# Another order of work for the second layer of an attention and two-layer network kernel on one Trainium2 core

## The chip, the core and the metric

The kernel runs on one core of a Trainium2 chip. The metric is the device time of one execution in microseconds (us), as the median of several runs.

## The reference

The program computes local attention with block summaries, a gated first layer, and a normalized second layer with a residual. Only the second layer (`_moe2_ref`) is touched by the change, and the tail of the first layer where the second one begins:

```python
def _moe2_ref(x, g_ln, w_ch1, w_ch2):        # x: (2, 768, 512), w_ch1: (512, 2048), w_ch2: (2048, 512)
    mu = np.mean(x, axis=-1, keepdims=True)
    var = np.mean((x - mu) ** 2, axis=-1, keepdims=True)
    xn = (x - mu) / np.sqrt(var + 1e-06) * g_ln
    ch = np.maximum(xn @ w_ch1, 0.0) @ w_ch2
    return (x + ch).astype(np.float32)
```

## The kernel before

All work is cut into 1932 operations (`Plan.op`). A table at the head of the file, `ORDER`, gives them in one list: a number names the operation, the letter behind it its engine (P TensorE, V VectorE, A ScalarE, G GpSimd, S the queue that issues DMAs). `Plan.trace` (L128) writes the instructions out in that order, so each engine runs its operations strictly as they follow in the list, and waits where an input or a buffer is not ready. Nothing else sets the order. Numbers in fp32 are split into a high and a low part, and each product of two matrices is made from three matmuls (high by high, low by high, high by low).

The second layer goes in 16 steps: step n takes one of the two batches and one of eight slices of 256 hidden columns (`steps`, L1055). A step has two halves.

- **First products** (`step`, L1251; `product`, L1257; matmuls at L1264). The 512x256 slice of the first weight is multiplied with the normalized input by a scheme of seven half-size products in place of eight, numbered 0 to 6. Each is six matmuls of 384 columns into one PSUM bank named `ch`. There are two such banks. Each product is taken out of its bank by VectorE (`plus`, L1273, instructions at L1275, sums into the tiles `p` and `u`). Product 0 is only copied out (L1297, by VectorE at L243 or by ScalarE at L241, as the list says), and product 4 is read twice. A bank is free for the next product when its readers are done.
- The sums go through a relu (`block`, L1280): ScalarE writes the high part of `cb` (L1284), VectorE the low part (L1287).
- **Second products** (`accum`, L1308; matmuls at L1342). `cb` is multiplied with 256 rows of the second weight: six tiles of 128 tokens, six matmuls of 512 columns each, summed over the steps of a batch in six PSUM banks `acc`. At the end of a stretch of steps VectorE adds them to the residual (L1351); the very last tile is done in two pieces (L1326, L1333).

Beside these run the weights: each slice is loaded in raw form (`raw`, two buffers, L1067), made fp32 by VectorE (L619, L628) and ScalarE (L623), scaled (L1094, L1096), summed (L1108), and split into high (ScalarE, L1120 to L1142) and low (`low`, L1073, L1075, GpSimd or VectorE). At the start of the layer the last tiles of the first layer come out of PSUM with their row sums (ScalarE, L803), the negated means are made (L245 or L241), ScalarE squares the rows (L810), and `ln_stats` (L1040) makes the scale: VectorE L1044, GpSimd L1047, VectorE L1049. Then the rows are normalized (`xn`, L1167 on ScalarE, L1170 on VectorE) and transposed by TensorE (L1205) for the second batch. A "row" below is a run of products of one kind that follow each other on TensorE.

Of the kernel before, what the change touches and what calls it, by code (L numbers as in the profile page):

```python
# [41 lines left out]
1236V 1246P 1199A 1198V 1237A 1072V 1200V 1250P 1140A 1247V 1201A 1141V 1238V 1143P 1211A 1203V 1142P 1204A 1215V 1248A 1254P 1205V 1155A 1249V 1144A 1206V
1277P 1156A 1145V 1207V 1255A 1146V 1149A 1279P 1209V 1208V 1213A 1210G 1251V 1219S 1212A 1148V 1217G 1158P 1150V 1252A 1157P 1151A 1147V 1278P 1253V 1153A
1152V 1170A 1216V 1256P 1214A 1154V 1225S 1159A 1258P 1218G 1171A 1257V 1160V 1244A 1172P 1161V 1164A 1173P 1163G 1259V 1262P 1162V 1166A 1245V 1264P 1168A
1263V 1167G 1165V 1221A 1269P 1266V 1260A 1169G 1265V 1179A 1281P 1174A 1270V 1227A 1180V 1267A 1220V 1273P 1175V 1176V 1178G 1283P 1274V 1177V 1226V 1287P
1183A 1261V 1222V 1280P 1228V 1223A 1184V 1229A 1282P 1284A 1224V 1271A 1230V 1275A 1352S 1285P 1181A 1272V 1347S 1268V 1310P 1276V 1286V 1182V 1306P 1288V
1353V 1289A 1311V 1354A 1291P 1316P 1292V 1349A 1290V 1348V 1293P 1350V 1355V 1298P 1351G 1295V 1356A 1294V 1314P 1299V 1300A 1302P 1301V 1307V 1318P 1361A
1365V 1357V 1312P 1319A 1303V 1359G 1358V 1304A 1360G 1362A 1320P 1315V 1296A 1366V 1326P 1305V 1398S 1297V 1403S 1342P 1321V 1313V 1327V 1328P 1308P 1329V
1400A 1330V 1364A 1399V 1322P 1317V 1368G 1337P 1323V 1324A 1344P 1338V 1331A 1401V 1363A 1339A 1404V 1346P 1367G 1325V 1402A 1405A 1333P 1406V 1343P 1309V
# [20 lines left out]
1912P 1879V 1892P 1913P 1893V 1884P 1898P 1885V 1894A 1903P 1900V 1901A 1916P 1904V 1895V 1905A 1899V 1914P 1906V 1907P 1922P 1908V 1909A 1915P 1910V 1902V  # L70
1911P 1920P 1924P 1921V 1918P 1925V 1926P 1919V 1917V 1930P 1923V 1928P 1927V 1931V 1929V
"""


# [1363 lines left out]
```

## Time and profile before

| what | value |
|---|---|
| median of 3 runs | 471.58 us (471.5 to 471.64) |
| the profiled execution, its own time | 471.01 us |
| its span from the first to the last instruction | 469.3 us |
| TensorE, matmuls | 460.1 us busy, 98% |
| VectorE | 352.4 us, 75% |
| ScalarE | 253.8 us, 54% |
| GpSimd | 140.6 us, 30% |

In the profile, PE is TensorE's matmuls and PEld its weight loads, DVE is VectorE, ACT is ScalarE, POOL is GpSimd. A matmul's time there is from its start to a modelled end; matmuls overlap, so what one costs is the distance from its start to the next one's start. A timeline row gives its start, its length, and in brackets the idle time ahead of it with what ended that.

### The profile page before, as it was taken

To read this page: it belongs to the slowest core of one execution; us is meant where nothing else is said; L and a number is where in the kernel's file an instruction comes from. 1 tells how busy PE (TensorE), PEld (TensorE's weight loads), DVE (VectorE), ACT (ScalarE), POOL (GpSimd) and SP (SyncE) were. 2 spreads that over 40 slices of the span, in tenths; PEclk is the share of its full clock that TensorE was granted. 3 is DMA by queue.
4 is the path that set the end of the run, shared out by engine and by line. 5 is a ranking of instruction groups with operands and counts; after the bars stand their busy time and mean duration, and the time that the engine had idled before them with its cause. 6 is when DMAs were issued, how large, how long until landed. Compare 5 with 4: busy or idle time off the path is not lost.

```text
span 469.3 us, 8641 instructions
## 1 busy us (share of the span) xinstructions
PE 460.1 (98%) x3212; PEld 405.9 (86%) x3212; DVE 352.4 (75%) x700; ACT 253.8 (54%) x665; POOL 140.6 (30%) x179
## 2 busy tenths in 40 slices
PE   8989999999999999999999999999999999999996
PEld 5548999888899989988889899999898998998985
DVE  3998998998767857998999874677655677654643
ACT  2898998957766666968953432232343234322010
POOL 5354245562425244231513321131131332102000
PEclk9999999999999999999999999999999999999999
DMA  8999976433002202002221041202222022110203
GB/s 231 315 243 260 237 186 159 98 70 81 10 18 47 92 1 89 2 0 91 91 91 54 36 135 53 83 14 77 89 91 88 3 89 90 45 46 0 104 32 134
DMA packets 56062, 43.16 MB, mean 92 GB/s; under 512 B 34393, under 2 KB 46965, under 8 KB 56021
## 3 DMA queue, kind: packets, MB, share of 16 engines
q1 hardware_dynamic: 55876, 42.55, 32.3%
q8 instruction: 25, 0.41, 0.4%
q14 instruction: 17, 0.13, 0.1%
q10 hardware_dynamic: 144, 0.07, 0.1%
HBM read 39.22 MB, written 3.15 MB: 90 GB/s over the span
## 4 chain that ended last, share of the span: by engine, by line
PE 88%; DMA 4%; DVE 2%; SPq 2%; ACT 1%; POOL 1%; issue 1%; POOLq 0%; ACTq 0%
PE acc L1342 27%; PE ch L1264 23%; PE x L794 12%; PE h L717 6%; PE tr L717 5%; PE ch L717 4%; PE tr L479 3%; PE h L794 2%; DMA wst<-in_moe_w_in_dram 2%; PE tr L562 2%; PE tr L463 2%; PE tr L343 1%; SPq L323 1%; POOL wi L640 1%; PE tr L455 1%
## 5 line engine op out<-in xcount | busy, mean ns | idle before, releaser
L1342 PE MATMUL acc<-w,cb 128*128 128x512 f32 x570 | 138.1, 390 | 0.0
L1342 PEld LDWEIGHTS acc<-w,cb 128*128 128x128 f32 x570 | 106.4, 188 | 18.5
L1264 PE MATMUL ch<-xb,w 128*128 128x384 f32 x384 | 75.2, 337 | 0.0
L1264 PEld LDWEIGHTS ch<-xb,w 128*128 128x128 f32 x384 | 67.9, 188 | 2.3
L1275 DVE TENSOR_TENSOR u<-ch,u 128x384 f32<-128x384 f32 x64 | 34.9, 552 | 30.5 <-PE ch L1264 29.8
L1264 PE MATMUL ch<-xt,w 128*128 128x384 f32 x288 | 57.0, 337 | 0.3 <-DVE u L1275 0.2
L747 DVE SCALAR_TENSOR_TENSOR c<-h,ccol,c 128x256 f32<-128x256 f32 (+1 forms) x80 | 49.6, 632 | 6.2 <-ACT c L241 3.6
L1264 PEld LDWEIGHTS ch<-xt,w 128*128 128x128 f32 x288 | 50.8, 188 | 2.9 <-DVE u L1275 1.1
L794 PE MATMUL x<-wo,ghi 128*128 128x512 f32 x160 | 50.6, 397 | 0.0
L1075 POOL TENSOR_TENSOR w<-raw,w 128x512 fp32r<-128x512 f32 (+1 forms) x16 | 20.1, 1258 | 80.6 <-ACT w L1142 75.4
L1284 ACT ACTIVATE cb<-p 128x384 fp32r<-128x384 f32 x32 | 16.5, 519 | 40.1 <-PE acc L1342 23.5
L623 ACT ACTIVATE raw<-raw 128x512 f32<-128x512 f32 x32 | 20.9, 671 | 27.2 <-DMA raw<-in_moe_w_ch_dram 23.0
L533 ACT ACTIVATE prob<-tr,nm 128x120 f32<-128x120 f32 x96 | 33.3, 368 | 2.4 <-DVE nm L521 1.6
L794 PEld LDWEIGHTS x<-wo,ghi 128*128 128x128 f32 x160 | 28.5, 189 | 3.8
L717 PE MATMUL h<-xT,wi 128*128 128x258 f32 x216 | 31.4, 290 | 0.0
L794 PE MATMUL x<-wo,glo 128*128 128x512 f32 x80 | 31.3, 392 | 0.0
L1284 ACT ACTIVATE cb<-u 128x384 fp32r<-128x384 f32 x32 | 16.1, 520 | 26.9 <-DVE u L1275 26.8
L717 PEld LDWEIGHTS h<-xT,wi 128*128 128x128 f32 x216 | 28.6, 191 | 1.6 <-issue 0.7
L717 PE MATMUL tr<-xT,wi 128*128 128x386 f32 (+1 forms) x168 | 28.8, 317 | 0.0
L717 PEld LDWEIGHTS tr<-xT,wi 128*128 128x128 f32 x168 | 26.4, 189 | 1.0 <-issue 0.2
L628 DVE SCALAR_TENSOR_TENSOR raw<-raw 128x512 uint32<-128x512 uint32 x32 | 21.7, 692 | 1.0 <-ACT raw L623 0.5
L1142 ACT CAST w<-raw 128x512 fp32r<-128x512 f32 x16 | 10.3, 655 | 21.3 <-DVE raw L628 21.3
(193 smaller groups left out, 838.1 us busy)
## 6 DMA issues: line engine op xcount, KB each, us to landing
raw<-in_moe_w_ch_dram SPq DMA_DIRECT2D x32, 512.0 KB, 3.8
wst<-in_moe_w_out_dram SPq DMA_DIRECT2D x8, 512.0 KB, 4.6
vw<-in_v_dram SPq DMA_DIRECT2D x20, 192.0 KB, 3.3
wst<-in_moe_w_in_dram SPq DMA_DIRECT2D x5, 512.0 KB, 7.2
s_q<-in_q_dram SPq DMA_DIRECT2D x8, 256.0 KB, 5.3
early<-in_k_dram SPq DMA_DIRECT2D x6, 256.0 KB, 4.4
x2a<-in_moe_w_in_dram SPq DMA_DIRECT2D x3, 512.0 KB, 6.2
early<-in_v_dram SPq DMA_DIRECT2D x3, 512.0 KB
```

Source lines behind the costliest of these rows:

```text
L479: T.matmul(av[s_, h_ * 256 + p * 64:h_ * 256 + p * 64 + 64], vv[:, p, s_], ps[a][:, p, 64 * h_:64 * h_ + 64], start=True, stop=True)
L533: A.activation(out=pr[:, p, :], in_=sc[:, p * NK:(p + 1) * NK], func=AF.Exp, bias=nm[:, p:p + 1], scale=1.0, accum_out=sm[:, p:p + 1])
L623: A.activation(out=f, in_=f, func=AF.Prelu, scale=F64_SCALE, alpha=F64_SIGN)
L628: V.scalar_tensor_tensor(out=most, in0=most, scalar=3, in1=least, op0=ALU.logical_shift_left, op1=ALU.bitwise_or)
L717: T.matmul(live["h", i][:, 0:N + 2], w_[:, c, f * 128:(f + 1) * 128], x_[:, c, 0:N + 2], start=(k_ == 0 and c == 0), stop=(k_ == 2 and c = ...
L747: V.scalar_tensor_tensor(out=ct, in0=ht[:, kk:kk + N], scalar=ccol[:, kk * NF + f:kk * NF + f + 1], in1=ct, op0=ALU.mult, op1=ALU.add)
L794: T.matmul(x2ps[g, t], l[:, ts_], r[:, f, :], start=(f == 0 and j == 0), stop=(f == NF - 1 and j == 2))
L1075: lambda e: on[e].tensor_tensor(out=hi()[1], in0=from_(), in1=hi()[0].bitcast(F32), op=ALU.subtract),
L1264: T.matmul(bk[k], l[:, c, :], x_[:, c, :], start=j == 0 and c == 0, stop=j == 2 and c == 1)
L1275: lambda e: V.tensor_tensor(out=temp(to), in0=bk[k], in1=temp(x), op=ALU.add),
L1284: A.activation(out=half(0, r, y), in_=temp(src), func=AF.Relu)
L1342: T.matmul(acc[key], ct_[n][l][:, r, 128 * t:128 * t + 128], w2[s][k][:, r], start=first and j == 0, stop=done and j == 5)
```

## The change

The table `ORDER` is another one from operation 1092 of the list on; everything else in the file is the same, and no operation is added or dropped. 55 operations also change their engine, such as the copy of product 0 in eleven steps. On TensorE the first products of the whole layer stood in 53 rows of these lengths:

```
7 1 2 3 3 1 1 2 2 2 1 2 1 2 2 2 4 3 4 2 2 1 2 1 2 1 2 1 1 2 2 4 2 1 5 2 2 1 2 2 1 3 2 4 2 2 1 3 3 2 1 2 1
```

and stand now in 23:

```
7 1 2 3 2 2 2 8 7 7 7 7 7 7 6 3 5 2 4 8 6 8 1
```

The second products between them stood in rows of one to four (seven at the end), and stand now in rows of two to six, with one of twelve and two of nine. Two lines of the diff:

```diff
...
-1575V 1570V 1585P 1576A 1613V 1622S 1584P 1614A 1615G 1634P 1608G 1628S 1578P 1635A 1623V 1587P 1579V 1577V 1580A 1572A 1636P 1581V 1624A 1630A 1642P 1637V
...
+1605A 1609V 1604A 1608V 1636P 1638P 1611V 1618A 1579V 1619V 1620A 1580A 1642P 1653P 1613V 1614A 1575V 1621G 1615G 1581V 1576A 1635A 1637V 1639V 1577V 1727S
...
```

TensorE in step 8, where products 1 and 2 stood apart: `xt` and `xb` are halves of the normalized input (one product is three lines, of two matmuls each), `w_24..` the first weight, `w_30..` the second. Before:

```order
L1264 MATMUL ch<-xt_2472,w_2474 128x384 x2
L1264 MATMUL ch<-xt_2473,w_2474 128x384 x2
L1264 MATMUL ch<-xt_2472,w_2475 128x384 x2
L1342 MATMUL acc<-w_3005,cb_3937 128x512
L1342 MATMUL acc<-w_3006,cb_3937 128x512
L1342 MATMUL acc<-w_3005,cb_3938 128x512
L1342 MATMUL acc<-w_3005,cb_3937 128x512
L1342 MATMUL acc<-w_3006,cb_3937 128x512
L1342 MATMUL acc<-w_3005,cb_3938 128x512
L1264 MATMUL ch<-xb_2468,w_2474 128x384 x2
L1264 MATMUL ch<-xb_2469,w_2474 128x384 x2
L1264 MATMUL ch<-xb_2468,w_2475 128x384 x2
```

and now products 2, 3, 4 and 6 in the same place:

```order
L1264 MATMUL ch<-xb_2468,w_2474 128x384 x2
L1264 MATMUL ch<-xb_2469,w_2474 128x384 x2
L1264 MATMUL ch<-xb_2468,w_2475 128x384 x2
L1264 MATMUL ch<-xb_2470,w_2474 128x384 x2
L1264 MATMUL ch<-xb_2471,w_2474 128x384 x2
L1264 MATMUL ch<-xb_2470,w_2475 128x384 x2
L1264 MATMUL ch<-xt_2472,w_2474 128x384 x2
L1264 MATMUL ch<-xt_2473,w_2474 128x384 x2
L1264 MATMUL ch<-xt_2472,w_2475 128x384 x2
L1264 MATMUL ch<-xb_2470,w_2474 128x384 x2
L1264 MATMUL ch<-xb_2471,w_2474 128x384 x2
L1264 MATMUL ch<-xb_2470,w_2475 128x384 x2
```

A tile of second products (six lines with `acc`) stood between two first products; now six first products of the step follow each other, and twelve tiles of second products come behind them.

ScalarE where the second layer starts: `x2b` is what the first layer leaves, `junk` the squares, `w` the high part of the second weight. Before:

```order
L803 ACTIVATE x2b,mneg<-x_2799 128x512
L803 ACTIVATE x2b,mneg<-x_2805 128x512
L803 ACTIVATE x2b,mneg<-h 128x512
L1142 CAST w_3005<-raw 128x512 x2
L810 ACTIVATE junk,ssq<-x2b,mneg 128x512 x3
L623 ACTIVATE raw<-raw 128x512
```

and now:

```order
L803 ACTIVATE x2b,mneg<-x_2799 128x512
L803 ACTIVATE x2b,mneg<-x_2805 128x512
L241 ACTIVATE mneg<-mneg 128x1
L803 ACTIVATE x2b,mneg<-h 128x512
L1142 CAST w_3006<-raw 128x512
L241 COPY p_3011<-ch 128x384
L1142 CAST w_3006<-raw 128x512
L810 ACTIVATE junk,ssq<-x2b,mneg 128x512 x3
L623 ACTIVATE raw<-raw 128x512
```

One scaling of `mneg` (L241) and the copy of product 0 (`p<-ch`) have come from VectorE, ahead of the squares, and a normalization (L1167) has left.

VectorE now, in the row of seven that ends step 8 and makes most of step 9 (in time: products 5 of step 8 and 0, 1, 2, 3, 6, 4 of step 9):

```order
L628 SCALAR_TENSOR_TENSOR raw<-raw 128x512 x2
L1275 TENSOR_TENSOR u_4096<-ch,u_4096 128x384
L1287 SCALAR_TENSOR_TENSOR cb_4225<-u_4064,cb_4224 128x384
L1275 TENSOR_TENSOR u_4278<-ch,p_4276 128x384
L1275 TENSOR_TENSOR p_4276<-ch,p_4276 128x384
L1287 SCALAR_TENSOR_TENSOR cb_4225<-u_4096,cb_4224 128x384
L1275 TENSOR_TENSOR u_4284<-ch,u_4278 128x384
L1287 SCALAR_TENSOR_TENSOR cb_4225<-p_4125,cb_4224 128x384
```

Between two lines with `<-ch`, which empty a bank, at most one other instruction stands; the copy of step 9's product 0 is ScalarE's.

## Rows read from the trace of the kernel before

**Rows 1.** The page: busy time, share of the span and instructions of each engine.
```profile
PE 460.1 (98%) x3212; PEld 405.9 (86%) x3212; DVE 352.4 (75%) x700; ACT 253.8 (54%) x665; POOL 140.6 (30%) x179
```

**Rows 2.** Busy time by stretch: sum, PE, PEld, DVE, ACT, POOL, clock, DMA share, GB/s.
```profile
212.02:235.76 23.74, 22.82 (x127) 20.41 (x126) 21.98 (x51) 21.10 (x43) 9.14 (x7) 1.00 0.28 90
235.76:463.82 228.06, 228.06 (x1142) 206.50 (x1141) 150.72 (x287) 73.09 (x144) 43.31 (x39) 1.00 0.20 65
```

**Rows 3.** Groups of TensorE from 235.76 to 463.82 (busy us, mean ns | idle before).
```profile
L1342 PE MATMUL acc<-w,cb 128*128 128x512 f32 x547 | 132.4, 390 | 0.0
L1264 PE MATMUL ch<-xb,w 128*128 128x384 f32 x342 | 66.5, 336 | 0.0
L1264 PE MATMUL ch<-xt,w 128*128 128x384 f32 x252 | 49.6, 336 | 0.0
```

**Rows 4.** Timeline of TensorE, 364 to 375 us: start, length, engine, line, operation.
```profile
364.88 1.22 PE L1264 MATMUL ch<-xt,w 128*128 128x384 f32 x6
365.94 2.25 PE L1264 MATMUL ch<-xb,w 128*128 128x384 f32 x12
368.03 2.25 PE L1264 MATMUL ch<-xt,w 128*128 128x384 f32 x12
370.11 4.24 PE L1342 MATMUL acc<-w,cb 128*128 128x512 f32 x18
374.19 2.09 PE L1264 MATMUL ch<-xb,w 128*128 128x384 f32 x11
```

**Rows 5.** Timeline of TensorE, 217 to 232 us.
```profile
217.99 1.31 PE L1264 MATMUL ch<-xt,w 128*128 128x384 f32 x6
219.14 1.20 PE L1264 MATMUL ch<-xb,w 128*128 128x384 f32 x6
220.77 1.07 PE L1205 MATMUL acc<-ident,xn 128*128 128x128 f32 x8 [0.43 <-DVE xn L1170]
221.59 1.29 PE L1264 MATMUL ch<-xb,w 128*128 128x384 f32 x6
...
229.81 0.60 PE L1205 MATMUL acc<-ident,xn 128*128 128x128 f32 x4
230.60 0.66 PE L1205 MATMUL acc<-ident,xn 128*128 128x128 f32 x4 [0.19 <-ACT xn L1167]
231.01 1.29 PE L1264 MATMUL ch<-xb,w 128*128 128x384 f32 x6
```

**Rows 6.** Timeline of ScalarE, 212 to 215 us.
```profile
212.22 0.60 ACT L803 ACTIVATE x2b<-h 128x512 f32<-128x512 f32 x1
212.72 0.19 ACT L803 ACTIVATION_READ_ACCUMULATOR x2b<-h 128x1 f32 x1
```

**Rows 7.** Groups of ScalarE, whole span (busy us, mean ns | idle before).
```profile
L241 ACT COPY p<-ch 128x384 f32<-128x384 f32 x9 | 4.2, 469 | 4.8 <-PE ch L1264 4.8
L241 ACT ACTIVATE mneg<-mneg 128x1 f32<-128x1 f32 x7 | 1.4, 207 | 0.0
```

**Rows 8.** Timeline of VectorE, 216 to 221 us.
```profile
216.45 0.17 DVE L1044 TENSOR_SCALAR rs<-ssq 128x6 f32<-128x6 f32 x1 [0.28 <-ACT junk L810]
...
217.39 0.55 DVE L1275 TENSOR_TENSOR u<-ch,u 128x384 f32<-128x384 f32 x1
...
218.77 0.16 DVE L1049 TENSOR_TENSOR rs<-mneg,rs 128x6 f32<-128x6 f32 x1
...
220.09 0.54 DVE L1170 TENSOR_SCALAR xn<-x2b,mneg,rs 128x512 f32<-128x512 f32 x1
```

**Rows 9.** Timeline of GpSimd, the same stretch.
```profile
216.70 1.34 POOL L1047 TENSOR_TENSOR rs<-rs,mhalf 128x6 f32<-128x6 f32 x1 [5.01 <-DVE rs L1044]
```

**Rows 10.** Timeline of VectorE, 366 to 368 us.
```profile
366.19 0.56 DVE L1275 TENSOR_TENSOR u<-ch,p 128x384 f32<-128x384 f32 x1 [3.73 <-PE ch L1264]
366.67 0.55 DVE L1287 SCALAR_TENSOR_TENSOR cb<-u,cb 128x384 fp32r<-128x384 f32 x1
367.19 0.56 DVE L1275 TENSOR_TENSOR p<-ch,p 128x384 f32<-128x384 f32 x1
```

More of the change, by code (lines that the diff above doesn't have):

```diff
@@ L42 @@
[L42 to L49, printed above, removed]
@@ L70 @@
[L70 to L71 removed]
+1024V 1011A 1127P 1048A 1129V 1012G 999P 1036V 1037A 1134A 1049V 1038V 1130V 1025A 1026V 1131V 1000P 1133G 1120V 1050V 1001P 1013P 1051A 1014P 1132V 1138A
+1039G 1040V 1015P 1027P 1052V 1053A 1139V 894A 902A 1054V 1028P 1029P 1041P 1042P 1043P 1055P 1136A 898A 1186V 1194V 1056A 1059P 1060A 1057A 1063P 1197S
@@ new lines @@
+1188V 1135V 1231P 1064A 1195A 1232A 1233P 1061V 1137V 1239P 1065V 1196V 1189A 1066A 1234V 1240V 1241P 1062A 1058A 1235P 1190G 1199A 1246P 1070V 1071G 1243V
+1242V 1236V 1237A 1250P 1072V 1198V 1140V 1200V 1141V 1143P 1201A 1211A 1202S 1203V 1204A 1238V 1142P 1247V 1215V 1254P 1205V 1225S 1248A 1249V 1206V 1279P
+1149A 1144A 1145V 1277P 1207V 1148V 1209V 1155A 1208V 1255A 1278P 1156A 1210V 1213A 1146V 1217G 1212A 1151A 1147V 1251V 1152V 1153A 1216V 1154V 1252A 1158P
+1159A 1214A 1253V 1150V 1157P 1160V 1170A 1171A 1218G 1256P 1257V 1164A 1244A 1258P 1161V 1172P 1259V 1162V 1245V 1173P 1163G 1166A 1262P 1263V 1165V 1168A
@@ new lines @@
+1264P 1179A 1265V 1167G 1180V 1266V 1269P 1270V 1282P 1174A 1260A 1271A 1175V 1226V 1176V 1177V 1273P 1274V 1169G 1219S 1220V 1227A 1221A 1283P 1267A 1183A
+1280P 1228V 1222V 1281P 1184V 1285P 1261V 1229A 1287P 1230V 1223A 1224V 1272V 1308P 1275A 1178V 1268V 1276V 1312P 1306P 1284A 1181A 1182G 1286V 1288V 1289A
+1347S 1349A 1348V 1350V 1352S 1353V 1351V 1354A 1291P 1293P 1316P 1292V 1355V 1314P 1310P 1356A 1357V 1294V 1295V 1359V 1296A 1297V 1290V 1302P 1303V 1298P
+1317V 1299V 1361A 1304A 1305V 1300A 1318P 1301V 1319A 1320P 1321V 1358G 1326P 1398S 1403S 1360V 1365G 1327V 1363A 1311V 1322P 1323V 1362A 1328P 1330V 1366G
@@ new lines @@
+1367G 1337P 1343P 1342P 1345P 1341P 1307V 1324A 1325V 1331A 1309V 1364A 1405A 1404V 1400A 1315V 1399V 1313V 1406V 1407V 1329V 1401V 1346P 1344P 1402V 1408V
+1338V 1339A 1410V 1409V 1340V 1333P 1368G 1412A 1334V 1413A 1369P 1370A 1332V 1371P 1372V 1335A 1373P 1374V 1336V 1377P 1416G 1375A 1411G 1388P 1379P 1378V
+1380V 1394P 1389V 1390A 1397P 1420S 1422A 1393P 1415A 1421V 1381V 1382A 1395P 1426S 1427V 1376V 1414A 1392P 1428A 1423V 1424A 1391V 1429V 1384P 1425V 1444P
+1419V 1438S 1432S 1418V 1385V 1417G 1446P 1448P 1386A 1452P 1387V 1383V 1445A 1447V 1430A 1431V 1449V 1450A 1454P 1463P 1396P 1470P 1469P 1467P 1468P 1472P
@@ new lines @@
+1453V 1456V 1457A 1455V 1439V 1440A 1433V 1464V 1451V 1465A 1434A 1458V 1435V 1436A 1466V 1441V 1442A 1443V 1473P 1437V 1459P 1474A 1460V 1475P 1476V 1461A
+1462V 1477P 1478V 1537S 1538V 1539A 1542S 1544A 1481P 1482V 1483P 1484V 1485V 1488P 1540V 1489V 1543V 1502P 1471P 1479A 1486A 1487V 1506P 1490A 1491V 1496P
+1541A 1545V 1546V 1480V 1492P 1493V 1552A 1494A 1547G 1508P 1509A 1495V 1551A 1555G 1510P 1511V 1512P 1513V 1516P 1527P 1556V 1517V 1549V 1553A 1518P 1520V
+1519V 1548G 1550V 1504P 1528V 1503V 1507V 1554A 1500P 1498P 1499V 1514A 1521A 1515V 1529A 1523P 1524V 1530V 1593S 1505V 1594V 1558G 1557G 1559P 1561P 1560A
@@ new lines @@
+1562V 1525A 1526V 1595A 1563P 1564V 1588S 1590A 1616S 1567P 1569P 1568V 1610S 1578P 1589V 1591V 1596V 1522V 1497V 1536P 1592A 1597V 1598V 1571V 1534P 1585P
+1535P 1586P 1532P 1603A 1600G 1602A 1531P 1628S 1501V 1606V 1601V 1622S 1533P 1607V 1583P 1584P 1587P 1582P 1574P 1634P 1612A 1565A 1566V 1617V 1570V 1599G
+1605A 1609V 1604A 1608V 1636P 1638P 1611V 1618A 1579V 1619V 1620A 1580A 1642P 1653P 1613V 1614A 1575V 1621G 1615G 1581V 1576A 1635A 1637V 1639V 1577V 1727S
+1643V 1644P 1572A 1659P 1657P 1573V 1658P 1660P 1630A 1629V 1624A 1640A 1641V 1646V 1647A 1623V 1625V 1645V 1654V 1631V 1626A 1655A 1656V 1663P 1664A 1649P
@@ new lines @@
+1650V 1651A 1665P 1666V 1652V 1632A 1667P 1668V 1648V 1633G 1671P 1672V 1673P 1674V 1675V 1627V 1662P 1661P 1688P 1728V 1682P 1669A 1670V 1683V 1684A 1685V
+1676A 1698P 1678P 1732S 1734A 1679V 1680A 1690P 1692P 1733V 1735V 1696P 1729A 1730V 1699V 1731V 1741A 1745G 1693V 1681V 1677V 1736V 1737G 1689V 1739G 1686P
+1694P 1740G 1738V 1700P 1701V 1706P 1707V 1697V 1702P 1703V 1708P 1709V 1713P 1710V 1714V 1742A 1704A 1715A 1724P 1687V 1721P 1783S 1784V 1785A 1786V 1778S
+1779V 1716V 1780A 1781V 1749P 1717P 1723P 1725P 1705V 1774P 1711A 1782A 1792A 1712V 1800S 1746G 1726P 1744A 1748G 1787V 1793A 1797G 1718V 1691V 1750V 1695V
@@ new lines @@
+1719A 1743A 1720V 1775P 1747G 1751P 1788V 1796V 1757P 1752V 1758V 1759P 1790G 1761V 1760V 1753P 1754V 1755A 1722P 1773P 1806S 1756V 1802A 1791G 1789G 1801V
+1808A 1794A 1776P 1803V 1804A 1807V 1798V 1795A 1809V 1799V 1772P 1810A 1768P 1769V 1770A 1764P 1824P 1765V 1811G 1766A 1826P 1825A 1762A 1771V 1767V 1828P
+1832P 1827V 1834P 1843P 1805G 1848P 1829V 1830A 1777P 1763V 1850P 1833V 1836V 1835V 1844V 1839P 1845A 1846V 1831V 1812S 1818S 1820A 1853P 1840V 1841A 1855P
+1854A 1842V 1856V 1861P 1862V 1837A 1819V 1838V 1813V 1872P 1814A 1815V 1821V 1863P 1865V 1847P 1816A 1817G 1864V 1852P 1849P 1822A 1823V 1878P 1879V 1851P
@@ L72 @@
+1884P 1876P 1877V 1873V 1886P 1882P 1883V 1857P 1858V 1868P 1869V 1859A 1860V 1874A 1870A 1875V 1888P 1871V 1889A 1866A 1890P 1891V 1896P 1867V 1897V 1892P
+1893V 1894A 1903P 1898P 1900V 1899V 1880P 1911P 1916P 1907P 1881V 1904V 1905A 1906V 1895V 1887V 1913P 1922P 1918P 1923V 1919V 1917V 1912P 1885V 1901A 1908V
+1909A 1920P 1921V 1915P 1910V 1914P 1902V 1924P 1926P 1925V 1930P 1927V 1931V 1928P 1929V
 """
```

22 lines of the change are left out of this document (removed).

## The prediction

> **What bounds the kernel now.** I read the page first, then busy time by stretch, then the groups and the timelines. TensorE computes for 98% of the span; the next engine, VectorE, for 75% [rows 1]. So only two things can shorten the kernel: TensorE waits that vanish, or matmuls that follow each other more closely. The stretches split the second layer, whose first matmul starts at 212.02 us and whose last tile starts at 463.82 [rows 2]. From 235.76 on TensorE is busy for 228.06 of 228.06 us, and no group there has idle time ahead of it [rows 2, 3]. All the layer's idle time on TensorE lies in the first 23.74 us, where matmuls cover 22.82 and VectorE and ScalarE are nearly full (21.98 and 21.10 us) [rows 2]. The granted clock is 1.00, the 2.4 GHz level, in both stretches, so the clock has nothing to give back. GpSimd and the DMA engines (a share of 0.20) are far from full. The new list can therefore gain where rows change in the long stretch, and gain or lose in the opening.
>
> **Rows of products: what a switch costs.** A product in the middle of a row takes 2.08 us / 2 = 1.04 (368.03 to 370.11), a plain tile of second products 4.08 / 3 = 1.36 (370.11 to 374.19) [rows 4]. The first product behind second products takes 1.06 (364.88 to 365.94) [rows 4]: 0.02 dearer. To price a whole alternation I use the sum. The groups count 594 matmuls of products and 547 of second products, which is 99 products and 91 tiles (with one matmul that only reaches in) [rows 3]. At the plain prices they take 99 x 1.04 + 91 x 1.36 = 102.96 + 123.76 = 226.72 us. The stretch is 228.06 and holds no idle time [rows 2], so 1.34 us are left. Of the 53 rows the first four (7, 1, 2, 3) hold the 13 products ahead of 235.76, so 49 rows lie in the stretch: 1.34 / 49 = **27 ns for a row**, that is for going over to products and back. By the timeline's 0.01 us the plain product may be 1.045 or the tile 1.355, which moves the price to 17 or 37 ns.
>
> The new list has the same first four rows in that count and 19 behind them in place of 49. 30 rows fewer x 27 ns = **-0.82 us**, bounds 30 x 17 = -0.51 and 30 x 37 = -1.11. All of it is on TensorE, which sets the end, so it counts in full if no wait takes its place.
>
> **What could take its place.** In a long row TensorE fills the two `ch` banks alternately, and VectorE must empty one while the other is filled. In the row of five, the product begun at 364.88 ends as the next begins at 365.94; its emptying runs from 366.19 to 366.75 [rows 10]; its bank is wanted again one product after 365.94, at 366.98. So 0.23 us are to spare in each product of 1.04. VectorE starts the next instruction 0.48 us after an emptying and the next emptying 0.52 after that [rows 10]: two instructions fill 1.00 of 1.04 us. One foreign instruction between two emptyings fits, a second does not. In the new VectorE order at most one stands there inside the long rows; product 4, read twice, is the last or last but one of its row, with a product or second products behind it before its bank is wanted; and eleven copies of product 0 change engine, in the example to ScalarE, which has 73.09 of 228.06 us in use [rows 2]. I cost the rows' waits at nothing. The cover is that 0.23 us; if it goes, see the second rival.
>
> **Second products, weights, other engines.** The tiles wait for `cb`. With longer rows a step's sums are complete in a lump, and up to twelve tiles follow, 12 x 1.36 = 16.3 us, while the rest of VectorE's work (low halves, weights) is made up. Its load in the stretch is 150.72 of 228.06 us [rows 2], so the mean leaves a third free. No work is added, and the weight loads keep their two `raw` buffers with DMA at 0.20 [rows 2]. The last tile's work is unchanged. I cost all this at nothing; what hides it is those tiles, and a late weight would stop TensorE outright, which falls under the same rival.
>
> **The opening.** Here waits move. ScalarE gets one scaling of `mneg` and the copy of product 0 ahead of the squares. By their means they last 0.21 and 0.47 us [rows 7]; starts follow each other some 0.10 us closer than lengths (0.60 long, next start after 0.50) [rows 6], so they delay the squares by about 0.2 + 0.37 = 0.57 us. `rs` at L1044 started at 216.45 when the last square was done [rows 8]; now about 217.0. Three followers:
> - VectorE's second emptying of product 4 ended at 217.39 + 0.55 = 217.94 and let product 5 start at 217.99 [rows 5, 8]. Behind the later `rs` and one emptying it starts at 217.03 + 0.24 + 0.48 = 217.75 (0.24 is a short instruction's start to start, an estimate) and ends at about 218.3: **product 5 +0.34**.
> - GpSimd's 1.34 us for the scale ended at 218.04 [rows 9], but VectorE took it up only at 218.77 [rows 8]. Now it ends at 218.6 and is taken up sooner, and the normalizations, one of which came from ScalarE, follow on VectorE. The transposes start at about 220.9 in place of 220.77 [rows 5]: +0.16, and that includes the 0.34, because they waited anyway.
> - The product after them (221.59) [rows 5] waits for an emptying that now stands behind more VectorE work: about 222.2, **+0.6**.
> Against this, the second transposes waited: two groups of four took 0.79 and 0.41 us (229.81 to 230.60 to 231.01) [rows 5], so 0.38 of idle time. The new list puts that normalization earlier on ScalarE, by enough to cover it: **-0.35**. Some 0.15 more of short waits and restarts go the same way (a product behind a wait took 217.99 to 219.14 = 1.15 in place of 1.04 [rows 5]). Net: +0.6 - 0.5 = **+0.1 us** at the product that started at 231.01. Bounds: -0.9 if the idle time (23.74 - 22.82 = 0.92 [rows 2]) all vanishes; +0.6 if nothing is given back.
>
> **Sum.** -0.82 + 0.1 = -0.72 us. The profiled execution took 471.01 with a span of 469.3, 1.71 around it; it would take 470.3 with a span of 468.6. It stands 0.57 below the median of 471.58, so the forecast for the median is 471.58 - 0.72 = **470.9**. By the bounds together: -0.51 + 0.6 = +0.1 to -1.11 - 0.9 = -2.0; I take -0.1 to -1.4 as this case's own range, since the two ends of the opening need every estimate to fail the same way. A measurement of this kernel can tell about 0.2%, 0.94 us.
>
> **Rivals.**
> *Switches are free.* The 1.34 us could be the plain prices' error, or waits too short to be listed, and then order changes nothing in a busy TensorE. Against it stands 1.06 behind second products beside 1.04 [rows 4]; for it, that this is the smallest digit of a timeline. Time: only the opening, +0.1, 471.7. The Trainium skill ("TensorE: Matmul & The Clock Gate", section on the back-to-back issue gap) gives an isolated gap that depends on the columns alone, N / 2.4 + 2.5 ns; by that a row costs nothing. The trace differs from it already in a plain tile, 1.36 / 6 = 227 ns for 512 columns where the page has 216. Chance 0.10.
>
> *Long rows starve on the two banks (slower).* If in a long row a second VectorE instruction falls between two emptyings (a low half late from ScalarE, a weight piece late from its load, so that it slips in among them), it takes 0.48 to 0.52 us against 0.23 to spare: TensorE waits about 0.28 and loses about 0.1 in the restart [rows 5, 10], 0.38 each time. Two such waits eat the saving of 0.82; five make the kernel slower by over 0.94 (5 x 0.38 - 0.72 = +1.2). One in each of the eleven rows of six or more behind the opening gives 11 x 0.38 - 0.72 = +3.5, 475.0; the point from which it decides is whether half of those rows have one. For it: emptyings and foreign work fill 1.00 of 1.04 us, and the list is fixed, so lateness is never made up by a swap. Against: the order shows no such pair where all is in time. The Trainium skill ("Perfetto Trace Analysis", section Optimization Strategy) says that interleaving regimes may help, and that the same gap recurring on the engine to be saturated can mean too few buffers for the next tile. By that, rows of one to four were the better ones; no row of before shows such gaps, since rows there are short. Chance 0.16.
>
> *The opening's waits vanish.* If ScalarE's earlier work costs VectorE less than I walked, the opening gives back most of its 0.92 us and restarts: about -1.2 in place of +0.1, so 469.6. For it: VectorE loses two instructions there. Against: the squares are later by 0.57. Chance 0.12.
>
> **How the numbers follow.** The forecast has 0.62, the rivals 0.10, 0.16 and 0.12. The time is the likeliest case's, 470.9 (own range 470.2 to 471.5). The range must reach over free switches (471.7) and the vanishing waits (469.6) and takes some milder starving (up to about four waits, +0.8): 469.6 to 472.4. Beyond lies most of the second rival. Faster by over 0.94 us (below 470.64): a third of the forecast's chance (0.21) and all of the third rival (0.12): 0.33. Slower (above 472.52): most of the second rival, 0.15. Within: 0.52.
>
> **What would show it.** Right: from the same product that started at 235.76, about 227.2 us to the last tile and still no idle time; the first product behind second products still 1.06; product 5 at about 218.3, the product behind the first transposes at 222.2, the one at 231.01 now near 231.1. Wrong: waits of TensorE for `ch` released by VectorE's L1275 inside rows of six to eight (second rival); a busy stretch of 228.0 with 19 rows (free switches); a start near 229.8 where 231.01 stood (third).

## The result and the profile after

The changed kernel took 474.32 us (median of 6 runs, 473.89 to 475.1) where before took 471.61 on the same chip: ratio 1.0059, 95% interval 1.0046 to 1.0072. It is **slower by 2.7 us**; the forecast was 470.9, the range 469.6 to 472.4.

The page of the changed kernel, engines' busy time, answers to [rows 1]:

```profile
PE 460.9 (98%) x3212; PEld 406.0 (86%) x3212; DVE 355.6 (75%) x705; ACT 255.6 (54%) x666; POOL 132.0 (28%) x173
```

It hides the loss: the shares are those of before. The stretches show it. I cut at the same work as [rows 2]: the layer's first product, the product that started at 235.76 before (now 238.96), and the last tile (now 466.67). Columns as there:

```profile
212.08:238.96 26.88, 23.48 (x127) 20.48 (x126) 23.72 (x49) 20.60 (x44) 9.62 (x7) 1.00 0.26 79
238.96:466.68 227.72, 227.71 (x1142) 206.03 (x1141) 153.29 (x294) 75.86 (x145) 36.30 (x33) 1.00 0.20 66
```

The first stretch grew from 23.74 to 26.88 us (+3.15 by the starts' nanoseconds), with matmuls in 23.48 of it: all of the loss. The second shrank from 228.06 to 227.72. The clock is the 2.4 GHz level in both. Now the places in the first stretch where TensorE waited: the list of its waits in the second layer, and its timeline from the product that [rows 5] begins with.

```profile
PE ch L1264 <- DVE u L1275: 1.6, 2, 0.9
PE acc L1205 <- DVE xb L1075: 0.9, 1, 0.9
PE ch L1264 <- ACT raw L623: 0.4, 1, 0.4
PE acc L1205 <- DVE xn L1170: 0.3, 1, 0.3
PE ch L1264 <- ACT p L241: 0.2, 1, 0.2
```

```profile
218.62 1.32 PE L1264 MATMUL ch<-xt,w 128*128 128x384 f32 x6 [0.69 <-DVE u L1275]
...
221.25 1.06 PE L1205 MATMUL acc<-ident,xn 128*128 128x128 f32 x8 [0.26 <-DVE xn L1170]
222.73 1.28 PE L1264 MATMUL ch<-xb,w 128*128 128x384 f32 x6 [0.41 <-ACT raw L623]
...
230.93 0.60 PE L1205 MATMUL acc<-ident,xn 128*128 128x128 f32 x4
232.39 0.63 PE L1205 MATMUL acc<-ident,xn 128*128 128x128 f32 x4 [0.86 <-DVE xb L1075]
233.09 1.32 PE L1264 MATMUL ch<-xb,w 128*128 128x384 f32 x6
234.24 1.25 PE L1264 MATMUL ch<-xt,w 128*128 128x384 f32 x6
236.43 1.34 PE L1264 MATMUL ch<-xt,w 128*128 128x384 f32 x6 [0.93 <-DVE u L1275]
```

Up to the product behind the first transposes the kernel is 1.1 us late (222.73 against 221.59 [rows 5]); the second transposes wait 1.0 more than their neighbours need, and the last product shown starts 2.18 us behind the one ahead of it in place of 1.04. What VectorE did at these two places, and GpSimd beside it:

```profile
229.10 0.95 DVE L1075 TENSOR_TENSOR xt<-ts,xt 128x768 fp32r<-128x768 f32 x1
229.97 1.66 DVE L1287 SCALAR_TENSOR_TENSOR cb<-u,cb 128x384 fp32r<-128x384 f32 x1
231.56 0.68 DVE L1075 TENSOR_TENSOR xb<-acc,xb 128x512 fp32r<-128x512 f32 x1
...
234.38 1.53 DVE L1287 SCALAR_TENSOR_TENSOR cb<-p,cb 128x384 fp32r<-128x384 f32 x1
235.83 0.54 DVE L1275 TENSOR_TENSOR u<-ch,u 128x384 f32<-128x384 f32 x1
```

```profile
229.85 1.37 POOL L1075 TENSOR_TENSOR w<-ss,w 128x512 fp32r<-128x512 f32 x1 [1.82 <-ACT w L1123]
...
234.20 1.29 POOL L1075 TENSOR_TENSOR xb<-sg,xb 128x512 fp32r<-128x512 f32 x1 [0.82 <-ACT xb L1239]
```

A low half (L1287) lasts 0.55 us where nothing holds it. These two lasted 1.66 and 1.53. Each began 0.1 to 0.2 us after a GpSimd instruction and ended 0.41 us after that one's end (229.85 + 1.37 = 231.22; 229.97 + 1.66 = 231.63). Behind the first stands the instruction that frees the transposes' PSUM bank (231.56), behind the second the emptying of a product (235.83), and for both of these TensorE waits. **Hypothesis:** a low half, whose two inputs both lie in SBUF, is held while GpSimd works, and what stands behind it on VectorE is late with it. Besides, ScalarE's squares end 1.0 us later: `rs`, which waits for the last of them, starts at 217.47 and not at 216.45 [rows 8].

```profile
217.47 0.17 DVE L1044 TENSOR_SCALAR rs<-ssq 128x6 f32<-128x6 f32 x1 [1.02 <-ACT junk L810]
217.55 0.56 DVE L1275 TENSOR_TENSOR p<-ch,u 128x384 f32<-128x384 f32 x1
```

### The profile page after: what moved, and what is told of

The parts are those of the page before. It is cut to its first block, busy times and chain, and to the rows that moved or that the text cites. A ratio compares the mean times of both kernels' runs of the same rounds, so it can differ in the third digit from the quotient of the medians.

```text
span 472.2 us, 8635 instructions
## 1 busy us (share of the span) xinstructions
PE 460.9 (98%) x3212; PEld 406.0 (86%) x3212; DVE 355.6 (75%) x705; ACT 255.6 (54%) x666; POOL 132.0 (28%) x173
## 3 DMA queue, kind: packets, MB, share of 16 engines
HBM read 39.22 MB, written 3.15 MB: 90 GB/s over the span
## 4 chain that ended last, share of the span: by engine, by line
PE 87%; ACT 3%; DMA 3%; DVE 2%; SPq 2%; issue 1%; POOL 1%; POOLq 0%; ACTq 0%
PE acc L1342 27%; PE ch L1264 23%; PE x L794 10%; PE h L717 6%; PE tr L717 5%; PE ch L717 4%; PE tr L479 3%; PE tr L562 2%; DMA early<-in_v_dram 2%; PE tr L463 2%; PE h L794 2%; PE tr L343 1%; DMA wst<-in_moe_w_in_dram 1%; ACT junk L810 1%; SPq L323 1%
## 5 line engine op out<-in xcount | busy, mean ns | idle before, releaser
L1342 PE MATMUL acc<-w,cb 128*128 128x512 f32 x570 | 132.7, 389 | 0.0
L1275 DVE TENSOR_TENSOR u<-ch,u 128x384 f32<-128x384 f32 x64 | 35.4, 553 | 19.9 <-PE ch L1264 19.1
L1075 POOL TENSOR_TENSOR w<-raw,w 128x512 fp32r<-128x512 f32 (+1 forms) x17 | 20.7, 1221 | 89.2 <-ACT w L1142 60.3
L1287 DVE SCALAR_TENSOR_TENSOR cb<-p,cb 128x384 fp32r<-128x384 f32 x32 | 20.5, 648 | 11.2 <-ACT cb L1284 11.2
L1287 DVE SCALAR_TENSOR_TENSOR cb<-u,cb 128x384 fp32r<-128x384 f32 x32 | 20.5, 644 | 5.9 <-ACT cb L1284 5.8
```

What stands on the lines that cost most here:

```text
L1075: lambda e: on[e].tensor_tensor(out=hi()[1], in0=from_(), in1=hi()[0].bitcast(F32), op=ALU.subtract),
L1275: lambda e: V.tensor_tensor(out=temp(to), in0=bk[k], in1=temp(x), op=ALU.add),
L1287: V.scalar_tensor_tensor(out=half(1, r, y), in0=temp(src), scalar=0.0, in1=half(0, r, y).bitcast(F32), op0=ALU.max, op1=ALU.subtract)
L1342: T.matmul(acc[key], ct_[n][l][:, r, 128 * t:128 * t + 128], w2[s][k][:, r], start=first and j == 0, stop=done and j == 5)
```

## Experiments

The table has, from each run's trace, the time from the layer's first product to the product that started at 235.76 us before (opening), from there to the last matmul's start (rest; 1.55 us behind the last tile's start in [rows 2]), and their sum; then the medians of the kernel and of before measured beside it, and the ratio with its interval. \* marks runs where one more tile of second products, 1.36 us, stands in the opening and not in the rest. Opening, rest and sum come from one profiled execution each; how far executions differ can be seen where lists agree: less that tile, e1 and e8 have the opening of before in 23.54 and 23.51 us (23.74), e2 the changed one in 26.73 (26.89). The intervals of all the repairs (e3 to e6, e10, e11) overlap the changed kernel's, so that a repair worked is read from the traces, not from the medians.

| run | opening | rest | sum | medians | ratio |
|---|---|---|---|---|---|
| before | 23.74 | 229.60 | 253.35 | | |
| changed | 26.89 | 229.26 | 256.15 | 474.32 / 471.61 | 1.0059 (1.0046 to 1.0072) |
| e1_rows | 24.90\* | 228.60\* | 253.50 | 471.50 / 471.29 | 1.0004 (0.9995 to 1.0014) |
| e2_opening | 28.09\* | 228.46\* | 256.55 | 475.17 / 471.29 | 1.0082 (1.0066 to 1.0098) |
| e3_swap | 25.34 | 229.49 | 254.83 | 473.23 / 471.29 | 1.0038 (1.0025 to 1.0050) |
| e4_gp | 26.08 | 229.27 | 255.35 | 473.68 / 471.29 | 1.0050 (1.0031 to 1.0070) |
| e5_pre | 26.21 | 229.34 | 255.55 | 473.86 / 471.67 | 1.0046 (1.0030 to 1.0061) |
| e6_pg | 26.80 | 229.33 | 256.13 | 473.93 / 471.67 | 1.0049 (1.0031 to 1.0068) |
| e8_best | 24.87\* | 227.93\* | 252.81 | 471.42 / 471.67 | 0.9994 (0.9984 to 1.0004) |
| e9_lock | 24.66 | 229.65 | 254.31 | 472.53 / 471.67 | 1.0010 (0.9999 to 1.0021) |
| e10_gp2 | 25.16 | 230.35 | 255.51 | 473.51 / 471.07 | 1.0051 (1.0037 to 1.0065) |
| e11_all | 24.47 | 230.29 | 254.75 | 472.97 / 471.07 | 1.0040 (1.0026 to 1.0054) |

### Which half of the list loses: e1 and e2

e1 is the list of before up to the cut with the changed list behind it (what is already done left out); e2 the other way round. One line of e1 against before, at the seam, where the two lists meet:

```diff
...
-1263V 1167G 1165V 1221A 1269P 1266V 1260A 1169G 1265V 1179A 1281P 1174A 1270V 1227A 1180V 1267A 1220V 1273P 1175V 1176V 1178G 1283P 1274V 1177V 1226V 1287P
+1263V 1167G 1165V 1221A 1269P 1266V 1260A 1169G 1265V 1179A 1281P 1174A 1270V 1227A 1180V 1267A 1220V 1282P 1271A 1175V 1226V 1176V 1177V 1273P 1274V 1283P
...
```

> The list of before up to the product that starts at 235.76 us, then the changed list: the long rows without the new opening. Theory (rows save, the opening loses): from that product to the last tile's last matmul start TensorE takes 229.26 us, as in the changed kernel, in place of 229.60, and nothing is lost ahead of it: 471.6 - 0.35 = 471.3 us. Rival (the long rows lose, the opening is innocent): about 474. Rival (rows free): 471.6, and the stretch 229.6.

> The other way round: the changed list up to that product, then the list of before. Theory (the opening loses 3.15 us): the product starts at about 238.9 us, the rest takes 229.6: 471.6 + 3.15 = 474.75 us. Rival (the long rows lose): about 471.6.

e2, with the rows of before, is no faster than the changed kernel (by the traces 3.20 us over before, where the changed kernel is 2.80 over): the opening carries the loss. e1 is level with before, not 0.35 us faster. Its trace says why: 0.61 us of waits at the seam, which neither parent has (0.49 where a normalized low half comes late, 0.12 behind it), and 0.30 in a long row. Less these 0.92 (0.917 by the nanoseconds) and with the tile put back, its rest is 228.60 + 1.36 - 0.92 = 229.04, that is 0.56 under before. By the medians no such saving can be told from nothing.

### Are the two held low halves on the path, and is GpSimd the holder: e3, e4, e9

e3 moves, on VectorE, the instruction that frees the bank ahead of the first low half, and the second low half behind the emptying:

```diff
-1159A 1214A 1253V 1150V 1157P 1160V 1170A 1171A 1218G 1256P 1257V 1164A 1244A 1258P 1161V 1172P 1259V 1162V 1245V 1173P 1163G 1166A 1262P 1263V 1165V 1168A
+1159A 1214A 1150V 1253V 1157P 1160V 1170A 1171A 1218G 1256P 1257V 1164A 1244A 1258P 1161V 1172P 1259V 1162V 1173P 1163G 1166A 1262P 1263V 1245V 1165V 1168A
```

> The changed list with two places of VectorE swapped in the opening: the instruction that frees the transposes' bank (L1075, at 231.56) ahead of the low half of 1.66 us (L1287, at 229.97), and the emptying of a product (L1275, at 235.83) ahead of the low half of 1.53 us (L1287, at 234.38). Theory (TensorE waits for what stands behind the two held low halves): the low halves still run long, the waits of 1.0 us ahead of the second transposes and of 1.1 us ahead of the product at 236.43 go: 474.3 - 1.6 = 472.7 us. Rival (all is late already because ScalarE's squares end 1.0 us later, the held low halves stand beside it): 474.3, within 0.3.

The opening shortens by 1.55 us, as the theory had it (1.6); 0.23 are lost again behind it, so the sum gains 1.3 and the median, compared through before, about 0.8. The low halves still lasted 1.06 and 0.96 us and ended 0.41 and 0.42 after GpSimd's instruction, but nothing that TensorE needed stood behind them.

e4 takes two operations, 1218 and 1167, from GpSimd (in each line one letter changes):

```diff
-1159A 1214A 1253V 1150V 1157P 1160V 1170A 1171A 1218G 1256P 1257V 1164A 1244A 1258P 1161V 1172P 1259V 1162V 1245V 1173P 1163G 1166A 1262P 1263V 1165V 1168A
-1264P 1179A 1265V 1167G 1180V 1266V 1269P 1270V 1282P 1174A 1260A 1271A 1175V 1226V 1176V 1177V 1273P 1274V 1169G 1219S 1220V 1227A 1221A 1283P 1267A 1183A
+1159A 1214A 1253V 1150V 1157P 1160V 1170A 1171A 1218V 1256P 1257V 1164A 1244A 1258P 1161V 1172P 1259V 1162V 1245V 1173P 1163G 1166A 1262P 1263V 1165V 1168A
+1264P 1179A 1265V 1167V 1180V 1266V 1269P 1270V 1282P 1174A 1260A 1271A 1175V 1226V 1176V 1177V 1273P 1274V 1169G 1219S 1220V 1227A 1221A 1283P 1267A 1183A
```

> The changed list with two instructions of the opening moved from GpSimd to VectorE (L1075, GpSimd at 229.85 for 1.37 us and at 234.20 for 1.29 us); VectorE has 2 x 0.6 us more to do. Theory (a low half with both inputs in SBUF is held while GpSimd works): the two low halves take 0.55 us in place of 1.66 and 1.53, VectorE is freed of 2.1 us and gets 1.2: the product at 236.43 starts about 1.4 us earlier, 472.9 us. Rival (they are long for another reason, such as late inputs): still over 1.2 us each, and VectorE's extra work makes it 474.3 to 475.5 us.

VectorE in e4, from the first of the two low halves on, GpSimd where it now meets the moved instruction, and TensorE's new wait:

```profile
230.42 0.55 DVE L1287 SCALAR_TENSOR_TENSOR cb<-u,cb 128x384 fp32r<-128x384 f32 x1
...
234.09 0.54 DVE L1287 SCALAR_TENSOR_TENSOR cb<-p,cb 128x384 fp32r<-128x384 f32 x1
...
236.09 1.43 DVE L1075 TENSOR_TENSOR xb<-sg,xb 128x512 fp32r<-128x512 f32 x1
```

```profile
235.11 1.85 POOL L1075 TENSOR_TENSOR xt<-ts,xt 128x768 fp32r<-128x768 f32 x1 [2.03 <-ACT xt L1239]
```

```profile
238.63 2.37 PE L1264 MATMUL ch<-xb,w 128*128 128x384 f32 x12 [0.76 <-DVE p L1275]
```

The hold is gone with GpSimd's instruction: 0.55 and 0.54 us. The last product of the opening comes 1.68 us earlier after the first (22.67 against 24.35). But the operation brought over has two SBUF inputs too and is now held itself beside the next GpSimd instruction (1.43 in place of 0.68), ahead of the emptying of product 4, and TensorE is 0.95 late there (a tile of 1.36 started at 236.32, the product behind it at 238.63). So half of the gain is lost again.

e9 makes the hold in the kernel of before, with nothing else changed: one low half goes behind the emptying that follows it.

```diff
-1152V 1170A 1216V 1256P 1214A 1154V 1225S 1159A 1258P 1218G 1171A 1257V 1160V 1244A 1172P 1161V 1164A 1173P 1163G 1259V 1262P 1162V 1166A 1245V 1264P 1168A
-1263V 1167G 1165V 1221A 1269P 1266V 1260A 1169G 1265V 1179A 1281P 1174A 1270V 1227A 1180V 1267A 1220V 1273P 1175V 1176V 1178G 1283P 1274V 1177V 1226V 1287P
+1152V 1170A 1216V 1256P 1214A 1154V 1225S 1159A 1258P 1218G 1171A 1257V 1160V 1244A 1172P 1161V 1164A 1173P 1163G 1259V 1262P 1162V 1166A 1264P 1168A 1263V
+1245V 1167G 1165V 1221A 1269P 1266V 1260A 1169G 1265V 1179A 1281P 1174A 1270V 1227A 1180V 1267A 1220V 1273P 1175V 1176V 1178G 1283P 1274V 1177V 1226V 1287P
```

> The list of before with one low half (L1287, VectorE at 232.14 us, 0.54 us long) moved behind the emptying that follows it, so that it comes to stand beside GpSimd's instruction at 232.75 us (1.30 us). Theory (it is held while GpSimd works): it takes over 1.0 us, what is behind it on VectorE is 0.6 us late, and the kernel takes 0.3 to 0.9 us more than before. Rival (no hold; the order of two VectorE instructions alone): 0.55 us, and the time of before within 0.2 us.

```profile
233.65 1.65 DVE L1287 SCALAR_TENSOR_TENSOR cb<-p,cb 128x384 fp32r<-128x384 f32 x1
235.22 0.68 DVE L1075 TENSOR_TENSOR xb<-acc,xb 128x512 fp32r<-128x512 f32 x1
```

```profile
233.58 1.30 POOL L1075 TENSOR_TENSOR xb<-sg,xb 128x512 fp32r<-128x512 f32 x1 [0.73 <-ACT xb L1239]
```

```profile
236.04 1.62 PE L1342 MATMUL acc<-w,cb 128*128 128x512 f32 x6 [0.82 <-DVE xb L1075]
```

1.65 us, again ending 0.42 behind GpSimd, and 0.97 more in the sum: by the profile's releaser the next second products wait for the instruction behind that low half on VectorE (L1075, at 235.22), which comes late with it. The medians are 0.86 apart; the interval of the ratio, 0.9999 to 1.0021, just touches no change.

### Is the late ScalarE the whole loss, and does lateness add up: e5, e6

e5 is the list of before up to the layer's first product, then the changed one (one line of three shown); e6 moves the emptying of product 5 ahead of two instructions.

```diff
...
-1188V 1135V 1231P 1064A 1195A 1232A 1233P 1061V 1137V 1239P 1065V 1196V 1189A 1066A 1234V 1240V 1241P 1062A 1058A 1235P 1190G 1199A 1246P 1070V 1071G 1243V
+1060A 1057A 1197S 1231P 1064A 1195A 1232A 1233P 1061V 1239P 1065V 1196V 1189A 1066A 1234V 1240V 1241P 1062A 1058A 1235P 1190G 1199A 1246P 1070V 1071G 1243V
```

> The list of before up to the layer's first product, then the changed list. ScalarE then reaches the last rows of the first layer as early as before; the scaling of mneg and the copy of product 0 are still ahead of the squares. Theory: rs (L1044) starts about 4.9 us behind the first product (4.4 before, 5.4 in the changed kernel), so half of the 1.0 us is of each origin; the product behind the first transposes comes 0.5 us earlier than in the changed kernel, but the low halves are still held by GpSimd, so at most 0.5 us comes through: 473.4 to 474.0 us where the changed kernel takes about 474. Rival (the late squares are the whole loss): 472.3 or less.

```diff
-1242V 1236V 1237A 1250P 1072V 1198V 1140V 1200V 1141V 1143P 1201A 1211A 1202S 1203V 1204A 1238V 1142P 1247V 1215V 1254P 1205V 1225S 1248A 1249V 1206V 1279P
+1242V 1236V 1237A 1250P 1072V 1198V 1140V 1200V 1141V 1143P 1201A 1211A 1202S 1247V 1203V 1204A 1238V 1142P 1215V 1254P 1205V 1225S 1248A 1249V 1206V 1279P
```

> The changed list with one emptying (L1275, for product 5, at 222.04 us) moved ahead of two other instructions of VectorE in the opening. TensorE's wait of 0.58 us behind the first transposes goes, and the product there starts 0.5 us earlier. Theory (the loss behind it is set by the held low halves): the product that started at 236.43 does not move by more than 0.2 us and the time stays within 0.2 us of the changed kernel. Rival (lateness adds up along TensorE): 0.5 us faster than the changed kernel.

In e5 `rs` starts 4.83 us after the first product (4.9 expected), and 0.68 us of the opening come back (at most 0.5 expected): the low halves are held there as well (1.66 and 1.54 us). So of the 0.96 us by which `rs` is later than before (5.39 against 4.43), 0.57 come from ahead of the layer, where the changed list has ScalarE do a cast (L1239, at 210.40 us) and a square (L810, at 210.91) just ahead of the last rows of the first layer (from 211.63 on; before, from 210.86), and 0.39 from the copy and the scaling. ScalarE in the changed kernel, ahead of the layer:

```profile
210.40 0.61 ACT L1239 CAST xb<-sg 128x512 fp32r<-128x512 f32 x1
210.91 0.72 ACT L810 ACTIVATE junk<-x2b,mneg 128x512 bf16<-128x512 f32 x1
...
211.63 0.58 ACT L803 ACTIVATE x2b<-x 128x512 f32<-128x512 f32 x1
```

e6 brings the product behind the transposes 0.57 us earlier, and the wait at the second transposes grows by 0.38; the opening as a whole gains 0.09. A wait taken away ahead of a held instruction was worth next to nothing here.

### All repairs together: e10, e11

e10 is e4 with the moved operation (1167) behind the emptyings of products 4 and 5. e11 is e5 with the edits of e10 and e6. Of e10 against the changed list, the line that differs from e4's:

```diff
...
-1264P 1179A 1265V 1167V 1180V 1266V 1269P 1270V 1282P 1174A 1260A 1271A 1175V 1226V 1176V 1177V 1273P 1274V 1169G 1219S 1220V 1227A 1221A 1283P 1267A 1183A
+1264P 1179A 1265V 1180V 1266V 1269P 1270V 1167V 1282P 1174A 1260A 1271A 1175V 1226V 1176V 1177V 1273P 1274V 1169G 1219S 1220V 1227A 1221A 1283P 1267A 1183A
```

> The changed list with the same two instructions moved from GpSimd to VectorE as in the run before with this edit, and the second of them (L1075, which was held itself for 1.43 us there, ahead of the emptying of product 4) behind the emptyings of products 4 and 5. Theory: both low halves take 0.55 us, and TensorE's wait of 0.95 us behind the tile of second products, new in that run, goes as well: from the layer's first product to the last tile 254.4 us by the trace (256.1 in the changed kernel, 253.3 before), about 1.0 us over before. Rival (VectorE has too much to do there in any order): no better than that run, 255.3 us.

> All three repairs at once: the list of before up to the layer's first product, then the changed list with the two instructions off GpSimd and behind the emptyings, and with the emptying of product 5 ahead of two other VectorE instructions. Theory (the three causes make up the loss and add up): 254.4 - 0.65 = 253.75 us from the first product to the last tile, 0.4 us over before; median within 0.2% of before. Rival (something of the opening's loss is still unnamed): over 254.4 us.

The opening does what the theory said: e10 takes 1.73 us off it, e5 alone 0.68, e11 2.42, which is their sum. The totals miss by 1.1 and 1.0 us, so the rivals' numbers come out, though for a reason that neither names: a product that lies in the rest now takes 2.32 us in place of 1.04. e10's TensorE and ScalarE:

```profile
242.24 0.51 PE L1264 MATMUL ch<-xt,w 128*128 128x384 f32 x2
243.59 0.93 PE L1264 MATMUL ch<-xt,w 128*128 128x384 f32 x4 [0.84 <-DVE xt L1075]
```

```profile
238.34 0.59 ACT L241 COPY sg<-acc 128x512 f32<-128x512 f32 x1 [3.07 <-DVE xb L1075]
```

The operation that I pushed back also frees the one buffer `sg`; ScalarE waits 3.07 us to refill it, and the normalized low half that comes out of that chain reaches TensorE late. What is left of e11's opening against before (24.47 - 23.74 = 0.73) starts behind the second transposes: until there e11 is level with or ahead of before (product 5 both 5.97 us after the first, the second transposes' last group 18.52 and 18.58), and then it waits for an emptying that stands behind the other operation brought over from GpSimd.

### The opening of before and the long rows, without the seam's waits: e8

e8 is e1 with two weight pieces ahead of one emptying on VectorE, so that the seam's waits go.

```diff
...
-1183A 1280P 1228V 1222V 1184V 1285P 1261V 1229A 1287P 1230V 1223A 1224V 1272V 1308P 1275A 1178V 1268V 1276V 1312P 1306P 1284A 1181A 1182G 1286V 1288V 1289A
+1280P 1228V 1222V 1274V 1184V 1285P 1261V 1229A 1287P 1230V 1223A 1224V 1272V 1308P 1275A 1178V 1268V 1276V 1312P 1306P 1284A 1181A 1182G 1286V 1288V 1289A
```

> The opening of before with the changed list behind it, and on VectorE two weight pieces (L628) ahead of one emptying (L1275), so that a normalized low half and a copy come earlier and the waits of 0.49 and 0.13 us at the seam go. Theory: 0.6 us less than without that move, so 0.45 us less than before: ratio 0.999. Rival (the waits come from something else, or move on): the same as without it, ratio 1.000.

The seam's waits are gone, and by the trace it is 0.54 us shorter than before and 3.3 shorter than the changed kernel. Against before the runs can't tell it from no change (0.9984 to 1.0004); it is clear of the changed kernel (1.0046 to 1.0072).

## Why the prediction was wrong

- **Rows of products.** Right in kind. The term was -0.82 us for 30 rows (bounds -0.51 to -1.11). Measured by the traces: the rest went from 229.60 to 229.26 with 0.30 of a new wait in it, so -0.64, or 21 ns for a row; e1 and e8, less their own waits, give -0.56 and -0.63. "Switches are free" does not fit: in the changed kernel a product behind second products takes 1.056 to 1.058 us, by the starts' nanoseconds, and most of those inside a row 1.040. The term came out smaller mostly because a product inside a row does not keep to 1.040: some take 1.048, and the mean is 1.044 over the 16 of before and 1.043 over the 58 of the changed kernel where nothing waits. With 1.044 the prediction's own sum would have left (1.34 - 99 x 0.004) / 49 = 19 ns.
- **Long rows starving on the two banks** (the slower rival). Not what happened: in ten of the eleven rows of six or more no product lost over 0.03 us. The one wait, 0.30 us in all, is in the eleventh, the last but one row: VectorE begins an emptying 0.35 us later than others of its kind, though idle and with its input there. That the kernel is slower, to which the prediction gave 0.15, does not bear this rival out, since the loss lies ahead of the long rows. The reading that at most one other instruction stands between two emptyings was wrong as it stood: in several rows two or three do, such as the three low halves ahead of the late emptying below. But between them ScalarE's copy of product 0 empties a bank, so VectorE has one product more.

```profile
442.93 0.56 DVE L1275 TENSOR_TENSOR u<-ch,u 128x384 f32<-128x384 f32 x1 [0.49 <-PE ch L1264]
443.40 0.55 DVE L1287 SCALAR_TENSOR_TENSOR cb<-p,cb 128x384 fp32r<-128x384 f32 x1
443.87 1.02 DVE L1287 SCALAR_TENSOR_TENSOR cb<-u,cb 128x384 fp32r<-128x384 f32 x2
445.41 0.56 DVE L1275 TENSOR_TENSOR u<-ch,p 128x384 f32<-128x384 f32 x1 [0.53 <-PE ch L1264]
```

- **The opening** is the step that failed: "+0.1 us at the product that started at 231.01", with bounds of -0.9 and +0.6, was +2.03 there (measured from the first product) and +3.15 at the end of the stretch. In its parts: the squares' delay of 0.57 was 1.02, since I walked ScalarE from 212 us on and took it to arrive there as early as before. Product 5 came at 218.62 (forecast 218.3), the transposes at 221.25 (220.9), the product behind them at 222.73 (222.2): 0.3 to 0.5 later, for the 0.45 that I had missed. It would have been more without two slips the other way: by my own rule (starts 0.10 closer than lengths) the scaling and the copy delay the squares by 0.11 + 0.37 = 0.48, not 0.57 (e5 shows 0.39), and the instruction behind `rs` came 0.08 after it, not 0.24. The -0.35 ("The new list puts that normalization earlier on ScalarE, by enough to cover it") failed outright. The normalization was in time, but the bank was not: its release stood behind a held low half, and the wait grew from 0.38 to 1.05. The second held low half cost 1.1 more.
- **The durations.** I priced each VectorE instruction by its usual length, so the sum had no term for a held one, and none of the three rivals names it. That "One foreign instruction between two emptyings fits" counts on 0.5 us; in the opening one of 1.53 stood there, and TensorE waited 0.93. Seven more low halves were held in the rest of the changed kernel, 0.74 to 1.58 us long, and TensorE waited behind none of them: what a hold costs goes by what stands behind it.
- **What the trace of before held.** It showed the price, and I passed over it: VectorE's and GpSimd's timelines of before at 264 us.

```profile
264.37 1.67 DVE L1287 SCALAR_TENSOR_TENSOR cb<-p,cb 128x384 fp32r<-128x384 f32 x1
```

```profile
264.04 1.58 POOL L1075 TENSOR_TENSOR w<-ss,w 128x512 fp32r<-128x512 f32 x1 [3.13 <-ACT w L1122]
```

It ends 264.37 + 1.67 - 264.04 - 1.58 = 0.42 us behind GpSimd. There it cost nothing, because nothing that TensorE waits for stood behind it.

In one sum: opening +3.15, of which repairs give back 0.68 for what stands ahead of the layer's start (e5) and 1.73 for the two held low halves (e10); the other 0.73 is not taken apart to the end, since e11 puts a new wait in the place of the old. No repair gives back the whole in the sum either: e11's is still 1.4 us over before. Rows -0.64, a late emptying +0.30: +2.8 in the trace, +2.7 in the medians.

## What to carry to other kernels

Before pricing a reordering, list the longest instances of each repeated instruction, not only its mean, and look at what the other engines did in them: a length that depends on the neighbour turns a harmless order into a wait. In a stretch where an engine is full (here VectorE, 21.98 of 23.74 us) ask of each instruction what stands behind it, and start the walk where the two lists part, not where the stage begins. A repair that moves work onto the full engine, or past the release of a single buffer, moves the wait rather than removing it.

## What the runs showed of the hardware

Counted over both traces from 205 us on: 15 low halves (L1287, two inputs in SBUF) started inside a GpSimd instruction with over 0.2 us of it still to go; they lasted 1.09 us on average before (6 of them) and 1.22 after (9), and every one ended 0.41 to 0.42 us behind GpSimd's end. The 99 that met no GpSimd instruction took at most 0.56 us. The 51 emptyings (L1275, one input in PSUM, one in SBUF) that started so took 0.55 us, the same as the others. The cleanest pair is L1075 on VectorE, one instruction in two places. Reading PSUM and SBUF (`xb<-acc,xb`) it took 0.67 to 0.68 us in all seven cases that started so; with both inputs in SBUF (`xb<-sg,xb`) it took 0.88 and 1.14 us in the two that did, and 0.68 where it met no GpSimd instruction. Two cases of the changed kernel, VectorE and then GpSimd beside it:

```profile
227.70 0.88 DVE L1075 TENSOR_TENSOR xb<-sg,xb 128x512 fp32r<-128x512 f32 x1
...
236.29 0.68 DVE L1075 TENSOR_TENSOR xb<-acc,xb 128x512 fp32r<-128x512 f32 x1
```

```profile
226.59 1.45 POOL L1075 TENSOR_TENSOR w<-ss,w 128x512 fp32r<-128x512 f32 x1 [7.53 <-DVE ss L1108]
...
235.45 2.16 POOL L1075 TENSOR_TENSOR xt<-ts,xt 128x768 fp32r<-128x768 f32 x1
```

So the hold goes by where the inputs lie. The other order is there too: in twelve cases the low half started first and took its usual 0.55 to 0.56 us; the GpSimd instructions (`w<-raw,w`) that started 0.12 and 0.16 us behind one (before, at 409 and 423 us) took 1.61 and 1.56 us, where alone they take 1.30 to 1.32. The Trainium skill ("SBUF — State Buffer", section Who interferes with whom) states this: a VectorE instruction with two SBUF inputs contends with a GpSimd instruction that reads SBUF, and the contention is an exclusive lock. The traces agree; where VectorE comes second they add that 0.41 of a low half's own 0.55 us is still to run when GpSimd ends.

Left open is the emptying that begins 0.35 us late in the last but one row (0.78 us after its product's last matmul start, 0.43 for others of its kind, `u<-ch,p`). It is there in e3, e5 and e6 at the same product, not in e4, e10 and e11, whose VectorE program is two instructions longer ahead of it; in e1 and e8 a like one, 0.79 and 0.81, stands at an emptying 157 us earlier. The profile names no releaser that came late. Counted over VectorE's records in the trace, semaphore instructions included, the late one is the 832nd in the changed kernel, e3, e5 and e6, and the 576th in e1 and e8: 256 apart, each right behind a semaphore instruction. That speaks for the place in VectorE's program and against a late input; what the engine does there no run shows.
